# A state-space convolution beside a gated product: half of the convolution's rows sent from SBUF to SBUF in place of a round trip through DRAM

## The chip, the core and the metric

The kernel runs on one core of one Trainium2 chip. The metric is device microseconds for one execution. TensorE (PE) multiplies into PSUM, ScalarE (ACT) and VectorE (DVE) evict and combine, GpSimd (POOL) does little, SyncE (SP) issues nearly all transfers, which run on 16 DMA engines.

## What is computed

The input is one sequence of 2,048 tokens with 512 channels, in bf16. After a layernorm, two branches run on it and are added to the input:

```python
def reference(A_u, A_A_re, ..., B_w_gate, B_w_up, B_w_down):
    ...
    # _A_ref: a long convolution per channel
    P = jnp.exp(logdA[:, :, None] * l[None, None, :])
    K = jnp.einsum("dn,dnl,dn->dl", Cc, P, dB).real      # D=512, N=128, L=2048
    ...                                                  # y = causal convolution of u with K, by FFT
    y = y + u * Dskip[None, None, :]
    # _B_ref: a gated product, F = 1792
    h = _sigmoid(x @ w_gate) * (x @ w_up)
    return h @ w_down
    ...
    return x + _A_ref(xn, ...) + _B_ref(xn, ...)
```

## The kernel before

*The gated branch* is cut into four groups of 512 tokens. For each group TensorE makes 14 gate blocks (L1010) and 14 up blocks (L1034), ScalarE applies the sigmoid (L1022), VectorE multiplies (L1049), and after a group's 14 products TensorE makes four down products of 128 tokens (L1078).

*The convolution* is done in a transformed space with matmuls. Each of its two halves of the channels (p = 0 and p = 1, 256 channels each) has eight units u. Of a unit: its input rows are loaded from DRAM (z_scr), transformed (L878) and evicted; the halves of the partitions are swapped (by four 64 KB copies big<-big for p = 0, by VectorE at L891 for p = 1); the filter's spectrum is made from a loaded table E (320 KB) and the kernel's rows kT (L900) and evicted; VectorE multiplies the two (L905, L909); TensorE transforms back in part (L922, called V here); ScalarE evicts the result into one of two buffers `vs` (L926, by the helper at L286). A helper (`dma`, L420) issues every transfer.

*The closing products* (`s2_mm`, L969, matmuls at L974 and L976) contract over 128 rows: 8 units x 4 rows x 4 blocks. They need these rows on the partitions, while `vs` holds 32 time positions x 4 blocks there. The change of layout is made by a store of each unit to DRAM (v_scr) and loads into the buffer `vall`. The stores go into three tensors (VPART: the first half; six units of the second half; its last two units), and for each of four parts of time there are three loads; a closing product waits for those of its part (`vp_op`). The results are added to the gated branch's (L989 and L1098) and stored.

*Order.* The kernel is recorded as 959 steps, each with an engine, its dependences and the buffers that it takes and frees. A list written out by hand, ORDER, says in which order the steps are issued; each engine and each queue works through its own steps in this order and stops at the first that has to wait. UEV says which up blocks ScalarE evicts ahead of the product, ON_DVE which copies VectorE makes in place of ScalarE. PSUM has two buffers of two banks (`pair`) and four of one bank (`bank`).

At the end of ORDER the last two units of the second half (u = 7, then u = 6) are followed by three gate and up blocks, and then by the down products 12 to 15 with the closing products between them.

Of the kernel before, what the change touches and what calls it, by code (L numbers as in the profile page):

```python
# [10 lines left out]
BF = mybir.dt.bfloat16  # L11
F32 = mybir.dt.float32
I32 = mybir.dt.int32
ACT = mybir.ActivationFunctionType
# [63 lines left out]
def _build_S2(by):  # L78
    h = np.zeros((64, 64))
    a = np.arange(64)  # L80
    h[0, :] = 1.0 / 2048
    h[1, :] = (-1.0) ** a / 2048
    for s in range(1, 32):
        h[2 * s, :] = 2.0 / 2048 * np.cos(2 * np.pi * s * a / 64)
        h[2 * s + 1, :] = -2.0 / 2048 * np.sin(2 * np.pi * s * a / 64)
    S2 = np.zeros((128, NA))
    S2[0:64] = h
    S2[64:128, 32:64] = h[:, 0:32]
    return S2.reshape(2, NU, 4, NA).transpose(1, 0, 2, 3)[by].reshape(128, NA)
# [88 lines left out]
def _consts():  # L178
# [19 lines left out]
UEV = (0, 1, 3, 5, 6, 7, 8, 10, 12, 16, 17, 19, 21, 22, 23, 24, 26, 27, 28, 29, 30, 31, 32, 33, 34, 35, 36, 37, 38, 39, 40, 41, 42, 44, 46, 49, 52, 54,)  # L198
ON_DVE = (66, 102, 103, 119, 120, 121, 135, 136, 137, 182, 192, 193, 195, 196, 228, 364,)
ON_ACT = (2,)  # L200
ORDER = [
# [115 lines left out]
def kernel(  # L317
# [80 lines left out]
    s2 = at(OFF["tmp"], [2, 64])  # L398
    rr = at(OFF["tmp"] + KB // 2, [D])
    sr = at(OFF["tmp"] + 3 * KB // 2, [4, 64])  # L400
# [6 lines left out]
    VPART = ((0, 0, NU // 2), (1, 0, NU // 2 - 2), (1, NU // 2 - 2, NU // 2))  # L407
    k_scr = dram.tile([16, NGE, 8, 2, NKQ * 16], BF, name="k_scr")
    c_scr = dram.tile([2, 16, 2, 16], BF, name="c_scr")
    v_scr = [dram.tile([4 * (u1 - u0), 128, DW], BF, name="v_scr%d" % n) for n, (p, u0, u1) in enumerate(VPART)]  # L410
# [332 lines left out]
    for c in range(4):  # L743
# [91 lines left out]
        def f_ds(pc=pc):  # L835
# [6 lines left out]
    kgen[3][0].rel += tuple(_Slot(k, i) for k, i in (("xx", 3), ("zx", 2), ("zx", 3), ("zx", 7), ("zx", 8), ("zx", 9)))  # L842
    kgen[2][0].rel += (_Slot("zx", 5), _Slot("zx", 6))
    gcs[3].rel += (_Slot("zx", 4),)
# [9 lines left out]
                vs=[OFF["kx"] + 4 * KB, OFF["kx"] + 6 * KB], zx=[OFF["zs"], OFF["zs"] + 2 * KB] + [KB * k for k in (4, 6, 12, 18, 20, 22, 28, 30)])  # L854
# [7 lines left out]
    v_st = [[] for _ in VPART]  # L862
    for p in range(NP):
        dsl = slice(DW * p, DW * p + DW)
        for u in UNITS[p]:
# [49 lines left out]
            def fv(u=u, sv=sv, pp=pp, pq=pq):  # L915
                for n in range(4):
                    q, y = n % 2, n // 2
                    for g in range(2):
                        ch = slice(DW * g, DW * g + DW)
                        for b in (0, 64):  # L920
# [6 lines left out]
            vn = [n for n, (p_, u0, u1) in enumerate(VPART) if p_ == p and u0 <= u < u1][0]  # L927
            vo = 4 * (u - VPART[vn][1])
            v_st[vn].append(dma("SP", v_scr[vn][vo:vo + 4, :, :].rearrange("g q d -> q g d"),
                               lambda vs=vs: vs().rearrange("p g y d -> p (g y) d"), deps=[ev], prio=QP - 1, rel=[vsl],  # L930
                               pkt=512)(256 * KB))

    TAIL = dict(ot=0, xt=8 * KB, glu=OFF["G"], vall=OFF["tmp"] - 32 * KB)
    assert TAIL["glu"] + 4 * KB <= TAIL["vall"]
    k_c = [dma("SP", c_scr[:][n], k_scr[:][:, 0, 0, :, 16 * (NKT - 1 + n):16 * (NKT + n)], deps=k_st[0] + k_st[1], prio=60, pkt=32)(1 * KB)
           for n in range(2)]
# [231 lines left out]
```

## Time and profile before

| | us |
|---|---|
| median of 3 runs | 222.95 (222.6 to 225.01) |
| the profiled execution, its own time | 223.55 |
| its span in the trace | 221.6 |
| PE busy | 206.1 (93%) |
| DVE busy | 198.9 (90%) |
| ACT busy | 176.3 (80%) |

The span runs from the first to the last instruction of the trace; 1.95 us of the execution's own time lie around it. The granted clock of TensorE was 0.99 over the span. Busy shares are averages over stages with different limits, so the views by time say more: rows of 40 slices have one digit for a slice of 5.54 us, in tenths of busy time. A wait is put down to what ended it last. Matmul rows have modelled ends and overlap each other.

### The profile page before, as it was taken

The page shows a single profiled execution, that of the slowest core. Times are in us where ns is not written, and L with a number is a line of the kernel's source. Part 1 is how long each engine was busy: PE and PEld are TensorE (multiplying, and loading weights), DVE is VectorE, ACT ScalarE, POOL GpSimd, SP SyncE. Part 2 cuts the span into 40 slices and gives each one's busy share as a digit, 9 for nine tenths or more (in the row PEclk, how much of TensorE's full clock was granted, in tenths as well). Part 3 has the DMA queues.
Part 4 walks back from the last instruction along what each step waited for, and adds up shares of the span by engine and source line. Part 5 has one row for each costly group of instructions (what it writes and reads, how often), then busy time and mean ns, then how long its engine had stood idle before and what let it go on. Part 6 is the DMA issues. An engine that isn't in the chain of part 4 may idle for free. (4 is left out here: it accounts for less than half of the span.)

```text
span 221.6 us, 4849 instructions
## 1 busy us (share of the span) xinstructions
PE 206.1 (93%) x1810; PEld 102.9 (46%) x1836; DVE 198.9 (90%) x440; ACT 176.3 (80%) x282; POOL 23.7 (11%) x40
## 2 busy tenths in 40 slices
PE   7769999999999999989999999999699999999694
PEld 2344444444444454435455565463347455544243
DVE  3899998999999999999999998999988999890663
ACT  3889999999999999849999999698486898851000
POOL 2101202005800000000000000004007400000000
PEclk9979999999999999999999999999999999999999
DMA  6999824005177476546595565879786999866934
GB/s 185 340 378 376 273 95 96 0 3 189 10 227 173 135 269 157 190 115 193 126 293 147 150 172 155 239 199 276 165 230 136 296 292 245 251 189 217 261 134 151
DMA packets 51529, 42.80 MB, mean 193 GB/s; under 512 B 16433, under 2 KB 43570, under 8 KB 51506
## 3 DMA queue, kind: packets, MB, share of 16 engines
q1 hardware_dynamic: 50338, 40.60, 61.6%
q0 software_dynamic: 864, 1.57, 4.4%
q10 hardware_dynamic: 304, 0.33, 0.5%
q8 instruction: 14, 0.23, 0.5%
q14 instruction: 9, 0.07, 0.1%
HBM read 25.97 MB, written 12.85 MB: 175 GB/s over the span
## 5 line engine op out<-in xcount | busy, mean ns | idle before, releaser
L286 ACT ACTIVATE big<-pair 128x1024 bf16<-128x1024 f32 x64 | 65.2, 1043 | 9.5 <-PE pair L878 3.2
L1034 PE MATMUL bank<-xnT,wu_sb 128*128 128x512 bf16 x215 | 54.0, 379 | 0.7 <-issue 0.2
L1010 PE MATMUL bank<-xnT,wg_sb 128*128 128x512 bf16 (+1 forms) x210 | 51.3, 376 | 2.4 <-ACT xnT L568 1.7
L1078 PE MATMUL bank<-wd_sb,hT_sb 128*128 128x512 bf16 (+1 forms) x232 | 49.7, 366 | 0.6 <-issue 0.2
L1010 PEld LDWEIGHTS <-wg_sb 128*128 128x128 bf16 x236 | 22.7, 100 | 26.5 <-issue 4.8
L1078 PEld LDWEIGHTS <-hT_sb 128*128 128x128 bf16 x238 | 22.8, 98 | 25.1 <-issue 1.7
L1022 ACT ACTIVATE hT_sb<-bank 128x512 bf16<-128x512 f32 x52 | 31.0, 625 | 2.0 <-PE bank L1010 1.9
L1034 PEld LDWEIGHTS <-wu_sb 128*128 128x128 bf16 x224 | 20.9, 98 | 25.0 <-issue 2.9
L731 DVE TENSOR_TENSOR big<-big 128x1024 bf16<-128x1024 bf16 (+4 forms) x40 | 26.8, 671 | 0.2
L732 DVE TENSOR_TENSOR big<-big 128x1024 bf16<-128x1024 bf16 (+4 forms) x40 | 26.7, 667 | 0.0
L1045 ACT ACTIVATE us_sb<-bank 128x512 bf16<-128x512 f32 x38 | 23.6, 625 | 0.3 <-PE bank L1034 0.3
L905 DVE TENSOR_TENSOR big<-big 128x2048 bf16<-128x2048 bf16 x16 | 19.5, 1218 | 1.6 <-DMA big<-big 0.8
L900 PE MATMUL pair<-big 128*128 128x256 bf16 x160 | 19.8, 273 | 0.1
L900 PEld LDWEIGHTS <-big 128*128 128x128 bf16 x160 | 15.6, 98 | 4.8 <-issue 0.2
L737 DVE TENSOR_TENSOR big<-big 128x512 bf16<-128x512 bf16 (+4 forms) x40 | 16.7, 417 | 0.0
L736 DVE TENSOR_TENSOR big<-big 128x512 bf16<-128x512 bf16 (+4 forms) x40 | 16.7, 416 | 0.0
L1049 DVE TENSOR_TENSOR hT_sb<-hT_sb,us_sb 128x512 bf16<-128x512 bf16 x38 | 15.8, 419 | 0.2 <-ACT hT_sb L1022 0.2
L785 ACT ACTIVATE sq_sb<-big 128x256 bf16<-128x256 bf16 (+2 forms) x20 | 13.5, 675 | 2.4 <-DVE big L737 2.4
L891 DVE COPY big<-big 32x1024 bf16<-32x1024 bf16 x32 | 14.5, 454 | 0.5
L922 PE MATMUL pair<-big 64*64 64x512 bf16 (+1 forms) x256 | 13.0, 326 | 0.5 <-ACT big L286 0.4
L1049 DVE TENSOR_TENSOR hT_sb<-hT_sb,bank 128x512 bf16<-128x512 bf16 x18 | 12.1, 684 | 1.4 <-PE bank L1034 1.1
L658 ACT ACTIVATE big<-big 128x512 bf16<-128x512 f32 x22 | 13.2, 681 | 0.0
(99 smaller groups left out, 222.9 us busy)
## 6 DMA issues: line engine op xcount, KB each, us to landing
big<-c_E SPq DMA_DIRECT2D x16, 320.0 KB, 4.3
z_scr<-big SPq DMA_DIRECT2D x16, 256.0 KB, 2.9
big<-z_scr SPq DMA_DIRECT2D x16, 256.0 KB, 4.1
v_scr<-big SPq DMA_DIRECT2D x16, 256.0 KB, 3.7
big<-in_A_u_dram SPq DMA_DIRECT2D x4, 512.0 KB, 9.4
big<-big SPq DMA_DIRECT2D x32, 64.0 KB, 3.5
big<-v_scr SPq DMA_DIRECT2D x4, 512.0 KB, 5.5
wu_sb<-in_B_w_up_dram SPq DMA_DIRECT2D x2, 896.0 KB, 11.0
```

Source lines behind the costliest of these rows:

```text
L286: nc.scalar.activation(out=get(out), in_=get(in_), func=ACT.Identity)
L731: V.tensor_tensor(out=wide(outp), in0=wide(lo), in1=mre, op=ALU.mult)
L732: V.tensor_tensor(out=wide(tb()), in0=wide(lo), in1=mim, op=ALU.mult)
L736: V.tensor_tensor(out=outp[:, :, 0], in0=outp[:, :, 0], in1=tb()[:, :, 1], op=opr)
L900: T.matmul(two(sk)[:, o:o + DW], es()[:, g, kt, :], kTv[p][:, :, kt, :], start=kt in (0, NKT - 1), stop=kt >= NKT - 2)
L905: V.tensor_tensor(out=pp().rearrange("p q h m -> p (q h) m"), in0=xx().rearrange("p q h m -> p (q h) m"), in1=kb()[:, 0:2 * DW].unsqueeze( ...
L1010: T.matmul(bank(sl, k % 2)[:, c0:c1], w[:, kt, k * 128:(k + 1) * 128], xnT[:, grp, kt, c0:c1], start=(kt == 0), stop=(kt == KT - 1))
L1022: S.activation(out=hT_sb[:, hs.idx, k % 2, :], in_=bank(sl), func=ACT.Sigmoid)
L1034: T.matmul(bank(sl), wu_sb[:, kt, k * 128:(k + 1) * 128], xnT[:, grp, kt, :], start=(kt == 0), stop=(kt == KT - 1))
L1045: S.activation(out=us_sb[:, us.idx, :], in_=bank(sl), func=ACT.Identity)
L1049: V.tensor_tensor(out=h(), in0=h(), in1=us_sb[:, us.idx, :] if on else bank(sl), op=ALU.mult)
L1078: T.matmul(bank(po)[:, 0:c[1] - c[0]], hT_sb[:, hts[k // 2].idx, k % 2, jj * 128:(jj + 1) * 128], wd_sb[:, k, c[0]:c[1]], start=first and ...
```

## The change

The second half's results no longer go through DRAM. After the eviction into `vs`, four copies of 64 KB for each unit, one for each pair of spectrum half and block (n = 0 to 3), go from SBUF to SBUF, straight to the buffer `vall` of the closing products: from 128 partitions with 512 bytes each into four partitions (32 n + 4 u and the three after it) with 16 KB each. Of the 32 copies 28 are issued by SP, four (the odd n of the last two units) by ScalarE's queue. The buffer `vs` is free again when all four have landed. The first half keeps its store and is loaded, as before, by four transfers of 512 KB, with the rows in another order; VPART is gone. The closing matrix S2 has its rows permuted to match. `vall` lies in another place, so the small tables s2, rr and sr move to `sq_sb`, and the list of buffers for the units' input rows (`zx`) is changed, with seven late places in place of eight. UEV, ON_DVE and ORDER are written anew; there are 975 steps. In ORDER no gate or up block is left behind the last unit; the load of the input rows for the last four results (512 KB, `lx`) is issued between the copies of the last two units.

```diff
-    return S2.reshape(2, NU, 4, NA).transpose(1, 0, 2, 3)[by].reshape(128, NA)
+    return S2.reshape(2, NU, 4, NA).transpose(1, 0, 2, 3)[by].reshape(NU // 2, 4, 4, NA).transpose(1, 0, 2, 3).reshape(128, NA)
...
-UEV = (0, 1, 3, 5, 6, 7, 8, 10, 12, 16, 17, 19, 21, 22, 23, 24, 26, 27, 28, 29, 30, 31, 32, 33, 34, 35, 36, 37, 38, 39, 40, 41, 42, 44, 46, 49, 52, 54,)
-ON_DVE = (66, 102, 103, 119, 120, 121, 135, 136, 137, 182, 192, 193, 195, 196, 228, 364,)
+UEV = (0, 2, 3, 4, 5, 6, 8, 13, 17, 19, 21, 22, 23, 24, 26, 27, 28, 29, 30, 31, 32, 33, 34, 35, 36, 37, 38, 39, 40, 41, 43, 44, 45, 46, 48, 50, 51, 52, 54, 55,)
+ON_DVE = (66, 81, 101, 103, 104, 119, 120, 135, 182, 194, 195, 196,)
...
-    s2 = at(OFF["tmp"], [2, 64])
-    rr = at(OFF["tmp"] + KB // 2, [D])
-    sr = at(OFF["tmp"] + 3 * KB // 2, [4, 64])
+    s2 = sq_sb[:, 0, 0:128].rearrange("p (r n) -> p r n", r=2)
+    rr = sq_sb[:, 0, 128:128 + D]
+    sr = sq_sb[:, 1, 0:256].rearrange("p (r n) -> p r n", r=4)
...
-    VPART = ((0, 0, NU // 2), (1, 0, NU // 2 - 2), (1, NU // 2 - 2, NU // 2))
...
-    v_scr = [dram.tile([4 * (u1 - u0), 128, DW], BF, name="v_scr%d" % n) for n, (p, u0, u1) in enumerate(VPART)]
+    v_scr = dram.tile([4, NU // 2, 128, DW], BF, name="v_scr")
...
-    kgen[3][0].rel += tuple(_Slot(k, i) for k, i in (("xx", 3), ("zx", 2), ("zx", 3), ("zx", 7), ("zx", 8), ("zx", 9)))
-    kgen[2][0].rel += (_Slot("zx", 5), _Slot("zx", 6))
-    gcs[3].rel += (_Slot("zx", 4),)
+    kgen[3][0].rel += tuple(_Slot(k, i) for k, i in (("xx", 3), ("zx", 2), ("zx", 3), ("zx", 4), ("zx", 5)))
+    kgen[2][0].rel += (_Slot("zx", 7), _Slot("zx", 8))
+    gcs[3].rel += (_Slot("zx", 6),)
...
-            vn = [n for n, (p_, u0, u1) in enumerate(VPART) if p_ == p and u0 <= u < u1][0]
-            vo = 4 * (u - VPART[vn][1])
-            v_st[vn].append(dma("SP", v_scr[vn][vo:vo + 4, :, :].rearrange("g q d -> q g d"),
-                               lambda vs=vs: vs().rearrange("p g y d -> p (g y) d"), deps=[ev], prio=QP - 1, rel=[vsl],
-                               pkt=512)(256 * KB))
-
-    TAIL = dict(ot=0, xt=8 * KB, glu=OFF["G"], vall=OFF["tmp"] - 32 * KB)
+            if p == 0:
+                v_st[0].append(dma("SP", v_scr[:, u].rearrange("g q d -> q g d"),
+                                   lambda vs=vs: vs().rearrange("p g y d -> p (g y) d"), deps=[ev], prio=QP - 1, rel=[vsl],
+                                   pkt=512)(256 * KB))
+                continue
+
+            for n in range(4):
+                r0 = 32 * n + 4 * u
+                v_st[1].append(dma("ACT" if n % 2 and u in (6, 7) else "SP", vall[r0:r0 + 4, 1].rearrange("p j i d -> p (j i) d"), lambda vs=vs, n=n: vs()[:, n // 2, n % 2, :],
+                                   deps=[ev] + table_free, prio=QP - 1, rel=[vsl] if n == 3 else [], pkt=512)(64 * KB))
...
-    vall = at(TAIL["vall"], [4, NP, 2, 4, DW])
+    v_v = v_scr[:].rearrange("g u (a j i) d -> (g u a) j i d", j=2, i=NT)
     vl = []
-    for t in range(0, 8, 2):
-        lds = []
-        for n, (p, u0, u1) in enumerate(VPART):
-            v_v = v_scr[n][:].rearrange("g q d -> (g q) d").rearrange("(p j i) d -> p j i d", j=2, i=NT)
-            lds.append(dma("ACT" if n == 2 and t % 4 else "SP", vall[16 * u0:16 * u1, t // 2, p], v_v[:, :, 2 * t:2 * t + 4, :],
-                           deps=v_st[n] + table_free, prio=20 + n + 0.01 * t, pkt=2048, hv=0.9)(64 * KB * (u1 - u0)))
-        vl.append(lds)
-    vp_op = [vl[t // 2] for t in range(8)]
+    for n in range(4):
+        vl.append(dma("SP", vall[:, 0, :, 4 * n:4 * n + 4], v_v[:, :, 4 * n:4 * n + 4, :], deps=v_st[0] + table_free, prio=20 + 0.02 * n, pkt=2048,
+                      hv=0.9)(512 * KB))
+    vp_op = [[vl[t // 2]] + v_st[1] for t in range(8)]
...
-            T.matmul(o[64 * j:64 * j + 64, :], s2[:, r, :], vall[:, t // 2, ps, j, 2 * (t % 2) + r, :], start=start, tile_position=(0, 64 * j), **kw)
+            T.matmul(o[64 * j:64 * j + 64, :], s2[:, r, :], vall[:, ps, j, i, :], start=start, tile_position=(0, 64 * j), **kw)
```

More of the change, by code (lines that the diff above doesn't have):

```diff
@@ L853 @@
                 pq=[OFF["lad"] + 10 * KB, OFF["pq"]],
-                vs=[OFF["kx"] + 4 * KB, OFF["kx"] + 6 * KB], zx=[OFF["zs"], OFF["zs"] + 2 * KB] + [KB * k for k in (4, 6, 12, 18, 20, 22, 28, 30)])
+                vs=[OFF["kx"] + 4 * KB, OFF["kx"] + 6 * KB], zx=[OFF["zs"], OFF["zs"] + 2 * KB] + [KB * k for k in (0, 2, 4, 6, 12, 18, 20)])
     mab = at(OFF["lad"] + 6 * KB, [NU, 2, 64])
@@ L860, in slot @@
         return sl, lambda: at(HOME[pool][sl.idx], shape)
-    v_st = [[] for _ in VPART]
+    TAIL = dict(ot=0, xt=8 * KB, glu=OFF["G"], vall=OFF["G"] + 8 * KB)
+    assert TAIL["vall"] + 32 * KB <= OFF["W0"]
+    vall = at(TAIL["vall"], [NP, 2, NT, DW])
+    v_st = [[], []]
     for p in range(NP):
@@ L926 @@
             ev = pl.copy(nc, 0.90, lambda vs=vs: vs().rearrange("p g y d -> p (g y d)"), lambda sv=sv: two(sv), [mv_], QP, acq=[vsl], rel=[sv])
-            vn = [n for n, (p_, u0, u1) in enumerate(VPART) if p_ == p and u0 <= u < u1][0]
-            vo = 4 * (u - VPART[vn][1])
-            v_st[vn].append(dma("SP", v_scr[vn][vo:vo + 4, :, :].rearrange("g q d -> q g d"),
-                               lambda vs=vs: vs().rearrange("p g y d -> p (g y) d"), deps=[ev], prio=QP - 1, rel=[vsl],
-                               pkt=512)(256 * KB))
-    TAIL = dict(ot=0, xt=8 * KB, glu=OFF["G"], vall=OFF["tmp"] - 32 * KB)
-    assert TAIL["glu"] + 4 * KB <= TAIL["vall"]
+            if p == 0:
[7 more added lines that the diff above has]
+                                   deps=[ev] + table_free, prio=QP - 1, rel=[vsl] if n == 3 else [], pkt=512)(64 * KB))
     k_c = [dma("SP", c_scr[:][n], k_scr[:][:, 0, 0, :, 16 * (NKT - 1 + n):16 * (NKT + n)], deps=k_st[0] + k_st[1], prio=60, pkt=32)(1 * KB)
```

87 rows, old and new, of the table ORDER are left out of this document.

## The prediction

> **What bounds the kernel now.** I read the page first, then the waits of TensorE (PE), the end of the chain, TensorE's order of time at the end, and the transfers by stretches. Durations are from the one profiled execution.
>
> ```profile
> span 221.6 us, 4849 instructions
> PE 206.1 (93%) x1810; PEld 102.9 (46%) x1836; DVE 198.9 (90%) x440; ACT 176.3 (80%) x282; POOL 23.7 (11%) x40
> PE   7769999999999999989999999999699999999694
> DVE  3899998999999999999999998999988999890663
> DMA  6999824005177476546595565879786999866934
> ```
>
> TensorE and VectorE are both nearly full until about 199 us; then VectorE is mostly idle and TensorE runs the closing products. From 140 us on the transfers are full too. The waits say what TensorE's few gaps are (total, times, longest):
>
> ```profile
> PE pair L974 <- DMA big<-v_scr: 2.0, 2, 1.5
> PE pair L878 <- ACT big L286: 1.7, 1, 1.7
> PE pair L878 <- DMA big<-z_scr: 0.9, 1, 0.9
> ```
>
> The first is the round trip this change removes; the chain shows it (start, us, what):
>
> ```profile
> 196.35 1.03 ACT big L286
> ...
> 197.39 4.22 DMA v_scr<-big
> ...
> 204.22 5.42 DMA big<-v_scr
> ...
> 209.80 2.97 PE bank L1078 x13
> ...
> 218.46 0.42 DVE big L1098
> ```
>
> The last unit's rows leave ScalarE at 197.38, are in DRAM at 201.61, and the last load lands at 209.64: 12.3 us. TensorE covers nearly all of it with down products:
>
> ```profile
> 198.60 0.39 PE L951 MATMUL pair<-ident,rz 128*8 128x128 bf16 x4
> 198.92 6.22 PE L1078 MATMUL bank<-wd_sb,hT_sb 128*128 128x512 bf16 x28
> 205.57 0.62 PE L974 MATMUL pair<-big 128*64 128x512 bf16 x4 [0.43 <-DMA big<-v_scr]
> ...
> 208.59 1.05 PE L974 MATMUL pair<-big 128*64 128x512 bf16 x8 [1.53 <-DMA big<-v_scr]
> ```
>
> So of 12.3 us only 0.43 + 1.53 + 0.16 (at 209.80) = 2.12 us are idle. That is all a shorter way can give at the end. Last, the transfers (last two columns: share of the 16 DMA engines, GB/s):
>
> ```profile
> 126.00:127.00 1.00, 0.95 (x18) 0.41 (x8) 1.00 (x6) 1.00 (x3) 0.00 (x0) 1.00 1.01 290
> 180.00:185.00 5.00, 4.95 (x57) 3.10 (x56) 4.76 (x10) 4.21 (x6) 0.00 (x0) 1.00 0.96 262
> 185.00:190.00 5.00, 4.95 (x55) 2.54 (x54) 4.86 (x10) 4.67 (x6) 0.00 (x0) 1.00 0.89 223
> ```
>
> In the first stretch nearly all packets are the 512-byte ones of one v_scr store: 16 x 512 B x 1.01 / 290 GB/s = 28.5 ns a packet on its engine. The other two show that the stage where the second half's units finish has almost no transfer time to spare.
>
> **The change, part by part.** *Removed:* eight 256 KB stores and 2 MB of reloads of the second half, and the 2.12 us of waiting. Span 221.6 - 2.1 = 219.5.
>
> *Order.* TensorE's instructions are the same set. By the list ON_DVE eight small steps move from VectorE to ScalarE and four the other way, and by UEV ScalarE evicts two more up products: VectorE loses about 1.6 us net (two products at 0.42 in place of 0.68, two layernorm applications at 0.31, one key eviction at 0.87, two small copies at 0.13, less a cast of 0.67), ScalarE gains about 2.8 us, which its 20% of idle time hides. I summed the work ahead of each step on its engine in both orders: the tightest VectorE-to-TensorE step has 0.7 us more room than before. One more product stands ahead of the first unit's spectrum product, two stand behind the last key table: these can cover the gaps of 0.9 and 1.7 us. Bounds: 0 to -2.6 us; I take 0 for the sum. In exchange no product is left between the last unit's matmul and the down products (before: three, 2.6 us).
>
> *Added:* each of eight units sends four copies of 64 KB, SBUF to SBUF, from 128 partitions x 512 B into **four** partitions x 16 KB. Issue: 28 on SP at 0.58 us (the row of the 32 copies big<-big) against 8 stores at 0.38 and six loads at 0.63 less; four on ScalarE's queue in place of two (0.66 to 0.99 us each there); two of these stand ahead of the last eviction, whose matmul comes 2.6 us later, so they are hidden. New waits: an eviction now waits for the four copies of the unit two before it (two vs buffers), with sigmoids and the other evictions queued behind it on ScalarE, and TensorE behind those for a PSUM pair. On SP the filter loads of the last two units (E, 320 KB) stand behind copies.
>
> No row shows a transfer into four partitions. Low end: 128 packets over 16 engines, 8 x 28.5 ns = 0.23 us a copy, landing about 2 us after issue as the copies into 32 partitions do in light traffic (105.97 to 108.05). High end: these copies into 32 partitions already pay: their 2 KB packets take a median of 147 ns (106.0 to 108.7 us, packet records), packets of that size into 128 partitions 84. By the same rate for each destination partition (64 KB in two rounds of 147 ns, 7 GB/s a partition) four partitions take 28 GB/s: 2.35 us a copy. I take one DMA engine for each destination partition, which lies between: 32 packets x 28.5 ns = 0.91 us a copy, **3.65 us a unit** on the same four engines, 29.2 us for eight, where the stores cost each engine 0.91 us a unit. The one-partition load in the trace (dskr, 1 KB) went as a single packet, so a transfer needn't use all engines.
>
> [...]
>
> **The sum.** The first copies are issued at about 175.6 (before: the first such store, 175.58). Ahead of the last copies the four engines must also do: what is queued already, about 3 us (transfers issued at 169 to 172 landed 7 to 8 us later); two E loads (8 packets of 102 ns each, 0.8 us each); two reloads of the first half (16 x 84 ns, 1.35 us each); the x load moved here (8 x 160 ns, 1.3 us); the SR load, 0.3. That is 8.9 us, and 29.2 for the copies: 213.7, landed 1.5 us later, 215.2. TensorE then has what it had from 205.57 on without its waits: 218.44 - 205.57 - 1.53 - 0.16 = 11.2 us, to 226.4; from there 3.1 us to the end (218.46 to 221.6): span 229.5, **7.9 us more**. The execution's own time was 223.55 for 221.6 of span, 231.5 for this one; the runs' median, 222.95, lies 0.6 lower, so 231. Own range: 226.5 (nothing queued, 27 ns packets) to 236 (5 us queued, queue at times empty).
>
> **Rivals.**
> - *Faster: the copies land like others.* Their price is the low end; TensorE's next step needs them at 198.6 + 0.39 + 6.22 = 205.2, they are there at about 203 (eviction to 199.7, two issues of 0.58, 2.0 to land). Span 219.5, 220.8 as a run; with the gaps of 0.9 and 1.7 closed 218.2. I take 220. It decides up to about 0.4 us a copy. For it: 512-byte packets take 27 to 28 ns whether loaded or stored, and there are 2 MB less to move. Against it: the 147 ns packets into 32 partitions.
> - *The partitions limit, not the engines.* The high end: 2.35 us a copy, 9.4 a unit, 75 for eight: 46 us more than above, 277; if two pairs of copies, into different quarters of the partitions, run side by side, half of 75: 8 us more, 239. For it: the same 147 ns. Against it: those copies also read only 32 partitions.
> - *The wait takes the removed one's place.* Price as for stores: landing 4.2 us after issue, behind the x load (1.3): 206.4 against 205.2 needed, so 1.2 us of the 2.1 come back: 222.
>
> [...]
>
> **How the numbers follow.** Forecast 0.36; copies harmless 0.25; partitions limit 0.32 (half of it side by side); replaced wait 0.07. A measurement of this kernel can tell about 1% from no change: below 220.7 is faster, above 225.2 slower. Faster: most of the harmless case, 0.21. Same: its rest, 0.04, and the replaced wait, 0.06: 0.10. Slower: 0.69. The range reaches from the harmless case with one gap closed, 218.5, to 262; beyond lies the serial half of the partitions' case.
>
> **What would show it.** Right: four-partition copies that land 5 us or more after issue, DMA share well under 0.9 while SP and ScalarE wait for them, L286 waiting for big<-big, TensorE idle before the last V products (L922's line) and before S2 (L974's), no wait longer than before ahead of 170 us. Wrong: copies landing in 2 to 3 us with TensorE unbroken from 199 us on; or new gaps before 170 us, which would make it the order.

## The result and the profile after

The changed kernel takes 260.7 us in the median (258.6 to 263.9) against 223.9 for the kernel before on the same chip: 1.161 times, interval 1.149 to 1.174. The forecast was 231: the direction holds, the loss is between four and five times as large (36.8 us in place of 8). Runs of one kernel differ by one or two per cent, the longer ones mostly at a lower granted clock, so the ratios leave the disturbed runs out, and the medians given beside them can lie a microsecond or two off.

The page of the profiled execution, to be read against the same rows of before (span 221.6, PE 206.1):

```profile
span 258.1 us, 4904 instructions
PE 217.3 (84%) x1836; PEld 106.6 (41%) x1836; DVE 197.4 (76%) x437; ACT 180.1 (70%) x287; POOL 21.5 (8%) x40
PE   7589999998999998999999998999909567830595
PEclk9869999999999999999999999999986955995589
DMA  6999340148713587877876877667464352446234
```

Up to about the 29th slice (187 us) TensorE is nearly as full as before. After it TensorE has holes, its granted clock drops (0.66 from 190 to 200), and the transfers take up half of the 16 engines' time (0.48 to 0.50 from 180 to 210). Before, the same stage looked like this (busy us of PE, PEld, DVE, ACT and POOL; last three columns: granted clock, share of the 16 DMA engines, GB/s):

```profile
180.00:190.00 10.00, 9.90 (x110) 5.64 (x110) 9.62 (x19) 8.88 (x12) 0.00 (x0) 1.00 0.93 243
190.00:200.00 10.00, 9.90 (x77) 4.98 (x78) 8.47 (x18) 6.21 (x9) 0.00 (x0) 1.00 0.75 231
200.00:210.00 10.00, 7.88 (x43) 3.48 (x43) 3.11 (x4) 0.59 (x1) 0.00 (x0) 1.00 0.79 235
```

A half-empty transfer row beside engines that wait for transfers needs a closer look. By the packet records, the 512-byte packets, nearly all of them the copies', fill 0.20 to 0.29 of the 16 engines in the 10 us stretches from 180 to 240, about four engines' worth (0.25). The waits in the changed kernel (total, times, longest; lines that do not bear on the copies left out):

```profile
...
ACT big L287 <- DMA big<-big: 22.3, 4, 8.1
...
DVE big L908 <- ACT big L287: 18.9, 4, 10.1
...
PE pair L976 <- DMA big<-big: 13.6, 1, 13.6
PE pair L925 <- ACT big L287: 10.0, 2, 6.7
...
PE pair L903 <- DMA big<-c_E: 4.2, 2, 3.7
```

big<-big is the copies. They hold TensorE at the closing products (L976), ScalarE at the evictions (L287: two row buffers, so an eviction waits for the copies of the unit two before), and through ScalarE TensorE again (L925) and VectorE (L908). The filter loads (c_E) are late behind them. The three TensorE waits are 27.8 us, of which before had 2.4; TensorE's busy time is 11.2 longer for the same products (217.3 against 206.1; 1,836 weight loads in both, though the trace of before lacks 26 of the matmul records). 27.8 - 2.4 + 11.2 = 36.6, nearly the 36.5 us between the two spans; the other waits come out about even. The chain that ended last shows the same: of the 59.3 us from 181.7 to 241.0, 40.7 are copies:

```profile
181.70 10.58 DMA big<-big
192.52 1.03 ACT big L287
...
200.61 12.52 DMA big<-big
213.27 1.03 ACT big L287
...
222.73 10.00 DMA big<-big
233.41 7.61 DMA big<-big
241.47 1.06 PE pair L976 x4
```

The stretches (last three columns: granted clock, share of the 16 DMA engines, GB/s) say where the extra busy time is:

```profile
190.00:200.00 10.00, 6.40 (x38) 3.17 (x37) 4.10 (x7) 6.02 (x8) 0.00 (x0) 0.66 0.49 99
200.00:210.00 10.00, 6.33 (x54) 3.33 (x54) 3.83 (x10) 2.35 (x4) 0.00 (x0) 0.78 0.48 77
210.00:220.00 10.00, 6.71 (x43) 2.34 (x41) 2.50 (x4) 2.92 (x4) 0.00 (x0) 0.54 0.30 58
220.00:230.00 10.00, 6.67 (x40) 2.94 (x32) 0.69 (x1) 3.12 (x4) 0.00 (x0) 1.00 0.50 83
230.00:240.00 10.00, 0.00 (x0) 0.00 (x0) 0.00 (x0) 0.00 (x0) 0.00 (x0) 0.64 0.58 78
240.00:250.00 10.00, 8.53 (x41) 4.23 (x43) 4.78 (x5) 0.00 (x0) 0.00 (x0) 0.67 0.32 116
```

Once TensorE begins to wait, the granted clock is 0.54 to 0.78 in four of the five stretches up to 240 and 0.67 in the next; before it was 1.00 from 180 to 210. Busy time times the clock that was not granted, summed over the stretches from 190 to 250, gives an estimate of 9.5 us, most of the 11.2. So the loss shows twice here: as idle time, and in slower products around it. Whether the waiting itself lowers the clock was not tested.

How many engines a copy uses can be estimated from the packets of four bytes that the traces hold. In the kernel with nothing but copies (below), four of them follow a copy into four partitions, and the 400 packets under 512 B on its page are what four for each such copy, eight for a copy into eight partitions and 16 for every other transfer add up to. That one such packet stands for one engine is the author's reading. The times of a copy into partitions four apart agree with it: its 128 packets of 28 ns are 3.6 us and were over in 0.9, four at a time. Before, after, and the later kernel with copies into eight partitions (one line of each page):

```profile
DMA packets 51529, 42.80 MB, mean 193 GB/s; under 512 B 16433, under 2 KB 43570, under 8 KB 51506
```
```profile
DMA packets 50377, 40.70 MB, mean 158 GB/s; under 512 B 16305, under 2 KB 43442, under 8 KB 50354
```
```profile
DMA packets 50505, 40.71 MB, mean 168 GB/s; under 512 B 16433, under 2 KB 43570, under 8 KB 50482
```

The change makes 16 more transfers. At 16 such packets each, as other transfers leave, the count under 512 B should rise by 256; it falls by 128, so the 32 copies leave 384 too few, 12 each: four engines a copy. Into eight partitions the count doesn't change (16433), so it is 8 too few for each copy: eight engines. Into 16 and into 32 partitions it rises by exactly 256 (16689): 16 engines.

### The profile page after: what moved, and what is told of

Read it like the earlier page. It is cut to its first block, busy times and chain, and to the rows that moved or that the text cites. A ratio compares the mean times of both kernels' runs of the same rounds, so it can differ in the third digit from the quotient of the medians.

```text
span 258.1 us, 4904 instructions
## 1 busy us (share of the span) xinstructions
PE 217.3 (84%) x1836; PEld 106.6 (41%) x1836; DVE 197.4 (76%) x437; ACT 180.1 (70%) x287; POOL 21.5 (8%) x40
## 2 busy tenths in 40 slices
DMA packets 50377, 40.70 MB, mean 158 GB/s; under 512 B 16305, under 2 KB 43442, under 8 KB 50354
## 4 chain that ended last, share of the span: by engine, by line
PE 39%; DVE 28%; DMA 19%; ACT 5%; POOL 2%; SPq 2%; issue 2%; ACTq 1%; DVEq 0%
DMA big<-big 16%; PE bank L1036 9%; PE bank L1012 8%; PE bank L1080 7%; DVE big L732 6%; DVE big L731 6%; PE pair L903 5%; PE pair L925 4%; DVE hT_sb L1051 4%; DVE big L737 3%; DVE big L736 3%; ACT big L287 2%; SPq L420 2%; PE pair L976 2%; POOL ln_ve_b L476 2%
## 5 line engine op out<-in xcount | busy, mean ns | idle before, releaser
L287 ACT ACTIVATE big<-pair 128x1024 bf16<-128x1024 f32 x64 | 65.0, 1033 | 32.0 <-DMA big<-big 22.3
L1036 PE MATMUL bank<-xnT,wu_sb 128*128 128x512 bf16 x224 | 56.1, 388 | 1.3 <-ACT big L287 1.3
L1012 PE MATMUL bank<-xnT,wg_sb 128*128 128x512 bf16 (+1 forms) x220 | 54.3, 389 | 1.1 <-ACT xnT L568 1.1
L1080 PE MATMUL bank<-wd_sb,hT_sb 128*128 128x512 bf16 (+1 forms) x238 | 50.5, 367 | 0.1
L908 DVE TENSOR_TENSOR big<-big 128x2048 bf16<-128x2048 bf16 x16 | 19.5, 1221 | 20.4 <-ACT big L287 18.9
L903 PE MATMUL pair<-big 128*128 128x256 bf16 x160 | 21.4, 288 | 4.3 <-DMA big<-c_E 4.2
L925 PE MATMUL pair<-big 64*64 64x512 bf16 (+1 forms) x256 | 14.4, 351 | 10.0 <-ACT big L287 10.0
L903 PEld LDWEIGHTS <-big 128*128 128x128 bf16 x160 | 16.4, 103 | 10.5 <-DMA big<-c_E 5.5
L976 PE MATMUL pair<-big,sq_sb 128*64 128x512 bf16 x24 | 6.6, 509 | 13.6 <-DMA big<-big 13.6
L991 DVE TENSOR_TENSOR big<-pair,big 128x1024 bf16<-128x1024 f32 x2 | 2.4, 1224 | 20.3 <-PE pair L976 20.1
L1051 DVE TENSOR_TENSOR hT_sb<-hT_sb,us_sb 128x512 bf16<-128x512 bf16 x40 | 16.7, 421 | 1.0 <-ACT us_sb L1047 0.9
L736 DVE TENSOR_TENSOR big<-big 128x512 bf16<-128x512 bf16 (+4 forms) x40 | 16.6, 416 | 0.1
L737 DVE TENSOR_TENSOR big<-big 128x512 bf16<-128x512 bf16 (+4 forms) x40 | 16.6, 415 | 0.0
L925 PEld LDWEIGHTS <-big 64*64 64x64 bf16 x256 | 7.3, 112 | 19.7 <-issue 16.7
```

Source lines behind the costliest of these rows:

```text
L287: nc.scalar.activation(out=get(out), in_=get(in_), func=ACT.Identity)
L736: V.tensor_tensor(out=outp[:, :, 0], in0=outp[:, :, 0], in1=tb()[:, :, 1], op=opr)
L737: V.tensor_tensor(out=outp[:, :, 1], in0=outp[:, :, 1], in1=tb()[:, :, 0], op=opi)
L903: T.matmul(two(sk)[:, o:o + DW], es()[:, g, kt, :], kTv[p][:, :, kt, :], start=kt in (0, NKT - 1), stop=kt >= NKT - 2)
L925: T.matmul(two(sv)[o:o + 64, DW * (2 * g + y):2 * DW * (g + 1)], mab[b:b + 64, 2 * u + g, q, :], pq()[b:b + 64, q, ch] if y else pp()[b:b ...
L1012: T.matmul(bank(sl, k % 2)[:, c0:c1], w[:, kt, k * 128:(k + 1) * 128], xnT[:, grp, kt, c0:c1], start=(kt == 0), stop=(kt == KT - 1))
```

## The experiments

**Order or copies?** Two halves of the change, each alone. First the new order, engine lists and buffers with the way through DRAM kept:

```diff
-  n in range(4): dma(vall[r0:r0 + 4, 1] <- vs[:, n])
+  dma(v_scr <- vs); later dma(vall <- v_scr)      # order, UEV, ON_DVE of the changed kernel
```

> The new order of work, the new lists of which engine evicts what and the new buffers, but the second half's rows go through DRAM as before the change: what the order costs by itself. Order theory (the copies are cheap, the new order is what costs): 250 us or more. Copies theory (any form of it): the changed kernel was only 2.6 us behind at its last key table, 158 us into the span, so 222 to 227 us, 0 to +1.5% against before. Middle: 225.

232.6 us, 1.043 (1.035 to 1.051): between what the two theories said, and what neither foresaw. The longest of TensorE's waits tells part of why:

```profile
PE pair L932 <- DMA big<-v_scr: 5.7, 2, 4.3
```

The new order has no product left between the last unit and the down products, so the DRAM trip that it does not expect to make stands open for 5.7 us in place of 2.0. That is 3.7 of the 8.8 us between the two spans; the rest is not explained here. This run prices the order with a transfer that it was not made for, not the order itself. The other half, the copies with the order and lists of before:

```diff
-UEV, ON_DVE, ORDER of the changed kernel
+UEV, ON_DVE, ORDER of the kernel before (copies put where the stores were)
```

> The opposite half: the copies of the changed kernel with the order and the engine lists of before. Copies theory: nearly the whole loss, 250 to 262 us. Order theory: 219 to 226 us. If the two only harm together: well under 250 here and under 227 in the run with the order alone.

261.7 us, 1.163 (1.145 to 1.181): the whole loss, with the order of before. The copies are the cause.

**Four partitions, or the copies as such?** The same number of copies, bytes and waits, spread wider:

```diff
-vall[r0:r0 + 4, 1]                          # r0 = 32 n + 4 u, 4 partitions x 16 KB
+vall[32 * n:32 * n + 32, 1][4 u: 4 u + 4]   # 32 partitions x 2 KB
```

> The changed kernel with each 64 KB copy going into 32 partitions x 2 KB in place of four x 16 KB: the same number of copies, bytes, waits and issues. The rows then land in another place of the buffer, so the closing products read other rows of the second half (same shapes, same instructions). Four-partition theories (either the four engines or the way into four neighbour partitions is the limit): the loss goes nearly all away, 221 to 230 us. Count-and-waits theory (32 more copies with their latency, two row buffers and an issue queue that waits in order): unchanged, 252 to 262 us. My forecast's price (0.91 us a copy on four engines becomes 0.23 on 16) would give about 222 to 226.

228.0 us, 1.014 (1.006 to 1.022). Count, issue and waits of 32 copies cost about 3 us; that each goes into only four partitions costs the other 33.

**Engines or partitions?** Four engines a copy either way, but partitions four apart:

```diff
-r0 = 32 * n + 4 * u;  vall[r0:r0 + 4, 1]
+vall[16 * u + n:16 * u + 16:4, 1]           # and rows of the first half and of the final sum to match
```

> The changed kernel with the rows numbered so that each copy still goes into four partitions, but into partitions four apart (r, r+4, r+8, r+12) in place of four neighbours; the first half's reloads go to every fourth partition, 512 KB each, the final sum reads its axes in the matching order. Engine theory (four engines carry each copy, whatever the partitions): unchanged within 2%, 255 to 263 us. Theory of a shared way into neighbour partitions: a copy is up to four times as fast, 222 to 235 us. Theory of a limit of each single partition: unchanged.

249.6 us, 1.119 (1.111 to 1.127), in the gap between the stated outcomes. The copies' 512-byte packets took 29 ns in the mean against 54 in the changed kernel, so neighbours do matter; but the reloads of the first half had become 16 KB packets (784 ns in the median), and TensorE's longest waits are put down to them (11.1 us at the filters' products). Repeated without that side effect:

```diff
-vall[r0:r0 + 4, 1]
+vall[16 * u + n:16 * u + 16:4, 1]           # nothing else
```

> The changed kernel with one edit: each copy goes into four partitions four apart (16u+n, +4, +8, +12) instead of four neighbours; the first half's loads stay as they are (in the run with partitions apart above they had become 16 KB packets of 0.6 to 1.7 us, which held the copies up). The closing products then read the second half's rows in another order; shapes and instructions are the same. In the changed kernel the copies' 512-byte packets take 54 ns in the mean, in the earlier run with partitions apart 29 ns. If the packets are 29 ns again and the four engines are the only limit, they need 29.7 us in place of some 55 for the copies: 25 us less, 232 to 238 us. If waits between the units set the pace: 245 to 252, as before. If partitions four apart gain only through the changed loads: 258 to 262.

234.6 us, 1.040 (1.031 to 1.048): some 26 of the 37 us are gone with the number of engines unchanged (16305 packets under 512 B, as in the changed kernel). Stretches and TensorE's waits of this kernel:

```profile
180.00:190.00 10.00, 8.76 (x81) 5.13 (x82) 8.58 (x15) 8.16 (x11) 0.00 (x0) 1.00 0.51 148
190.00:200.00 10.00, 7.33 (x77) 3.96 (x77) 5.81 (x15) 5.60 (x8) 0.00 (x0) 1.00 0.50 140
```
```profile
PE pair L976 <- issue: 4.2, 1, 4.2
PE pair L925 <- ACT big L287: 3.0, 2, 2.5
```

The transfer share is the same half as in the changed kernel, at about one and a half times the GB/s (148 and 140 in place of 93 and 99): as many engines, but each packet short (30 ns in the mean against 54). The wait at L976, from 210.3 to 214.5, is listed as "issue", but it is still the one for the copies: the semaphore that TensorE waits for gets its last four landings, those of the last copy, from 213.9 to 214.2. Then 16 and eight neighbours:

```diff
-vall[r0:r0 + 4, 1]
+vall[32 n + 16 (u % 2): + 16, 1][8 (u // 2): + 8]     # 16 partitions x 4 KB
+vall[32 n + 8 (u % 4): + 8, 1][16 (u // 4): + 16]     # other run: 8 partitions x 8 KB
```

> The changed kernel with each copy going into 16 neighbouring partitions x 4 KB (the closing products read the second half's rows in another order). Engine count as the limit: 16 engines as with 32 partitions, packets of 27 to 31 ns, 225 to 230 us. [...]

> The same with eight neighbouring partitions x 8 KB. Engine count alone (eight engines, 29 ns packets): 0.46 us a copy, 14.9 us for all 32, which the work between units hides: 226 to 231 us. Partitions alone (eight neighbours at twice the rate of four): half of the changed kernel's loss against the copies into 32 partitions, 240 to 246 us. [...]

228.9 us, 1.016 (1.009 to 1.023), and 241.2 us, 1.070 (1.061 to 1.079). Side by side:

| a copy goes into | engines | groups of four neighbours | ratio to before |
|---|---|---|---|
| 4 neighbours (the change) | 4 | 1 | 1.161 |
| 8 neighbours | 8 | 2 | 1.070 |
| 4, four apart | 4 | 4 | 1.040 |
| 16 neighbours | 16 | 4 | 1.016 |
| 32 neighbours | 16 | 8 | 1.014 |

Eight engines on two groups of neighbours do worse than four engines on four (1.070 against 1.040): how the partitions lie is the first limit. Counting in groups of four is the author's choice; no run tried two or three neighbours, and none shows what neighbours share. With four groups each, 16 engines gain 5.7 us over four (234.6 - 228.9): the engines are the second. (The four copies of a unit share one block of 16 partitions in the run four apart, and have a block each in the run with 16 neighbours, so this pair alone does not prove it; the run with nothing but copies bears it out.) The expectation for copy8p by engines alone (226 to 231) is refuted.

**The disputed cost by itself.** A kernel with nothing but copies, each waited for by a small VectorE step:

> No part of the computation but the copies: 64 KB from 128 partitions (512 bytes each), one at a time, three times over into four neighbouring partitions, four partitions four apart, 8, 16 and 32 neighbours, each waited for before the next is issued; then groups of four copies (a unit's) into four groups of neighbours in different quarters, into four partitions four apart within one block of 16, all four into the same four neighbours, and into 32 partitions each. From the changed kernel's packet records (97 to 121 ns a packet and 22 to 30 GB/s where one copy ran alone, 27 to 29 ns with partitions apart): four neighbours 2.2 to 3.0 us of packets (64 KB at 22 to 30 GB/s), four apart 0.9 us, 8 neighbours 1.1 to 1.5, 16 and 32 neighbours 0.25 to 0.7; four copies into the same four neighbours 9 to 12 us, into different quarters 3 to 9, four apart 3.7. If the neighbours are no limit by themselves and the long packets come from other traffic: 0.9 us for four neighbours too.

The steps of one round, in the order four neighbours, four apart, 8, 16 and 32 neighbours (in brackets, from the step before until the copy has landed):

```profile
39.94 0.30 DVE L340 COPY src<-dst 128x128 bf16<-128x128 bf16 x1 [4.46 <-DMA dst<-src]
42.79 0.30 DVE L340 COPY src<-dst 128x128 bf16<-128x128 bf16 x1 [2.54 <-DMA dst<-src]
46.31 0.30 DVE L340 COPY src<-dst 128x128 bf16<-128x128 bf16 x1 [3.22 <-DMA dst<-src]
49.09 0.30 DVE L340 COPY src<-dst 128x128 bf16<-128x128 bf16 x1 [2.48 <-DMA dst<-src]
51.66 0.30 DVE L340 COPY src<-dst 128x128 bf16<-128x128 bf16 x1 [2.27 <-DMA dst<-src]
...
80.57 0.30 DVE L340 COPY src<-dst 128x128 bf16<-128x128 bf16 x1 [12.08 <-DMA dst<-src]
86.00 0.30 DVE L340 COPY src<-dst 128x128 bf16<-128x128 bf16 x1 [5.13 <-DMA dst<-src]
99.18 0.30 DVE L340 COPY src<-dst 128x128 bf16<-128x128 bf16 x1 [12.88 <-DMA dst<-src]
103.72 0.30 DVE L340 COPY src<-dst 128x128 bf16<-128x128 bf16 x1 [4.24 <-DMA dst<-src]
```

The last four are groups of four copies: neighbours in four quarters, four apart, all into the same neighbours, 32 partitions. One copy more into neighbours costs (12.08 - 4.46) / 3 = 2.5 us, one more into partitions four apart (5.13 - 2.54) / 3 = 0.86. Nothing else ran, so other traffic is not the reason. The packet records of the groups: 87 to 101 ns a packet and 25.6 to 28.1 GB/s for neighbours, 28 ns and 76 to 78 GB/s four apart. 28 ns is what 512-byte packets take elsewhere in these kernels (27 to 28), so four apart the four engines work without a gap and are the limit.

**A dose.** Half the copies:

```diff
-for n in range(4):
+for n in (0, 2):
```

> The changed kernel without the copies n = 1 and 3 of each unit: 16 copies in place of 32 (half of the second half's rows are not moved, all waits on the others stay). If the four engines are a queue that always has work, what the copies cost is their engine time: half of 55 us, 27.5, about what 32 copies into partitions four apart took (29.7 us, 234.6): 231 to 237 us. If the waits from unit to unit set the pace (an eviction waits for the copies of the unit two before it): 245 to 256, since each unit still waits for two slow copies. If only the other traffic slows them: 245 to 255 too.

238.5 us in the median of four runs (232.9 to 239.9), too few to give an interval. That is well below what waits from unit to unit were expected to give (245 to 256); the shortest run lies within what a queue that always has work gives (231 to 237), the others 1 to 3 us above. The cost goes mostly with the number of copies. But each unit also waits for two copies in place of four here, so the two theories are not fully told apart.

**What a harmless copy is worth.** Copies into 32 partitions with the order of before:

```diff
 ORDER, UEV, ON_DVE of the kernel before
+vall[32 * n:32 * n + 32, 1][4 u: 4 u + 4]
```

> The copies into 32 partitions x 2 KB with the order and engine lists of before (closing products read the second half's rows in another order): what a harmless copy would be worth. My forecast's first rival: the 2.1 us of waiting at the end go, 0.985 to 0.995 of before. If the new order costs nothing and the three microseconds seen with it come from the copies: 1.01 to 1.02, as with the new order. If the copies still collide with the loads: 1.00 to 1.03.

227.0 us, 1.015 (1.010 to 1.020), the same as with the new order (1.014), so between the two orders no difference can be seen once the transfer fits them. But the copies are not harmless even here. TensorE's waits, then its closing part and the copies on SP's queue:

```profile
PE pair L860 <- DMA big<-c_E: 3.1, 2, 1.9
...
PE pair L882 <- ACT big L244: 1.5, 2, 0.8
```
```profile
203.74 6.22 PE L1037 MATMUL bank<-wd_sb,hT_sb 128*128 128x512 bf16 x28
209.89 0.62 PE L933 MATMUL pair<-big,sq_sb 128*64 128x512 bf16 x4
```
```profile
176.05 6.18 SPq L377 DMA_DIRECT2D big<-big  x8
182.33 0.53 SPq L377 DMA_DIRECT2D big<-c_E  x1
...
185.61 7.11 SPq L377 DMA_DIRECT2D big<-big  x8
```

The waits of the closing products are gone, as forecast: they follow the down products at once. But the down products start at 203.74 where they started at 198.92: 4.8 us later, 3.1 of them in waits for filters (c_E) and 1.5 for evictions. Eight copies hold SP for 6 to 7 us, and the filter loads stand behind them. The span is 224.4, 2.8 over before: 4.8 lost, 2.0 regained. Moving two filter loads ahead of the copies:

```diff
-u4.copies, u1.copies, ... u5.E, reload 2, u6.E, u7.E
+u5.E, u6.E, u4.copies, u1.copies, ... u7.E, reload 2
```

> The copies into 32 partitions with the order of before, and on SP's queue the filter loads of the two last-but-one units moved ahead of the first eight copies and one 512 KB reload of the first half moved behind the last filter load. In the run without this TensorE waits 1.2 and 1.9 us for these filters, which were issued up to 7 us later behind the copies. If that is where the remaining 3 us (1.015) went: 0.995 to 1.005 of before. If the transfers as a whole are the limit (the wait only moves): 1.01 to 1.02.

227.7 us, 1.010 (1.006 to 1.014), at the lower end of the second stated outcome (1.01 to 1.02). The waits for filters are no longer among TensorE's longest, and the one for evictions (L882) has grown from 1.5 to 3.3:

```profile
PE pair L882 <- ACT big L244: 3.3, 3, 2.4
```

The wait mostly moves. Whether half a per cent was won can't be said, since the intervals overlap.

**A version that beats both?** Only the last units by copies, everything else as before:

```diff
+if u in (6, 7): n in range(4): dma(vall[16 u + 4 n: + 4, 1] <- vs[:, n])    # neighbours
```

> The kernel before, with its order, where only the last two units of the second half go by four copies each into four neighbouring partitions and the other six keep the way through DRAM; result complete. By my forecast's price (0.91 us a copy) the last copy lands about 203, before TensorE needs it at 205.2, and the 2.1 us of waiting go: 0.99 of before. At the price seen in the changed kernel (54 ns a packet, 1.7 us a copy, 6.9 us for the last unit's four from 198 on, landing at 206 to 207): 0.99 to 1.00. With the unit before it still in the queue: 1.01 to 1.03.

232.4 us, 1.033 (1.026 to 1.039), just above the worst of the three outcomes. Eight copies hold SP from 199.1 to 206.7, the last reloads stand behind them, and those end last:

```profile
PE pair L938 <- DMA big<-v_scr: 6.6, 1, 6.6
```

Then only the very last unit, into partitions four apart:

```diff
+if last unit: n in range(4): dma(vall[96 + n:112:4, 1] <- vs[:, n])
```

> The kernel before, with its order, where the very last unit of the second half alone goes by four copies, into four partitions four apart; all others keep the way through DRAM (the first half's store of the unit with that number is cut into four of 64 KB). Result complete. Copied alone, such a group of four took 5.1 us from issue to landing in the run with nothing but copies, so from 197.4 to about 202.5, before TensorE needs it at 205.2: the 2.1 us of waiting go, 0.985 to 0.995 of before. If the copies queue behind the loads still open on their four engines (some 1.4 MB, 4 us): 206 to 207, 0.995 to 1.005. If the other loads now end last because they are issued 2.3 us later: 1.00 to 1.01.

227.8 us, 1.016 (1.009 to 1.022): no gain, and above all three stated outcomes. The copies themselves are in time (their last packets end at 202.3); the reloads of the other units, issued from 199.92 on in place of 197.80, are now what TensorE waits for:

```profile
197.40 2.48 SPq L380 DMA_DIRECT2D big<-big  x4
199.92 7.10 SPq L380 DMA_DIRECT2D big<-v_scr  x5
```
```profile
PE pair L946 <- DMA big<-v_scr: 1.8, 1, 1.8
```

The profile is of the shortest of its six runs (224.2 us), whose span of 222.3 is only 0.7 over before; the median says 3 us, and where the others lose the rest was not found. No version tried beats the kernel before.

## Why the prediction was wrong in size

- *The term that failed: 0.91 us a copy, "one DMA engine for each destination partition, 32 packets x 28.5 ns".* No row of before shows one engine for each partition, always the same four, nor the 1.5 us to landing. The engines came out right: by the four-byte packets four a copy, and four copies four apart together still moved about four packets at a time (512 of 28 ns in the 3.4 us that 256 KB take at 76 to 78 GB/s). From the last copy's last packet to its landings it took 0.2 to 0.5 us four apart, 2.2 to 2.5 with neighbours. The 28.5 ns were wrong: they came from a store to DRAM, and with four neighbours as destination the packets took 54 ns in the mean in the kernel, 87 to 101 in the kernel with copies alone. Copies ran from about 180 to 240 us, 60 us for 32 or 1.9 each, where the sum had 29.2 us. TensorE could go on at 241.5 in place of the sum's 215.2, and from there to the end took 16.6 us in place of 14.3, at a granted clock of 0.67 at first: 26.3 + 2.3 is the whole difference between the span of 258.1 and the sum's 229.5.
- *The rest of the sum came out, in part by luck.* With partitions four apart, where 30 ns a packet were measured, the sum's last copy "landed 215.2" and its span of 229.5 met 214.5 (when TensorE goes on) and 230.1. So the working fits another layout: a limit of the destination was left to the second rival. But the sum put the whole loss into one wait ahead of the closing products, from 205.2 to 215.2; in that run TensorE waited only 4.2 us at this place and had lost the rest earlier: its down products began at 204.3 in place of 198.9. The queue of the copies set the end either way.
- *The second rival had the price, but not the unit.* Its 2.35 us a copy, from the 147 ns packets into 32 partitions, is nearly the 2.5 us measured alone. It spoke of a rate for each destination partition (7 GB/s); four partitions four apart took 76 to 78 GB/s together, four neighbours 25.6 to 28.1, so what limits is that they are neighbours. The time came between its two ends (239 and 277): in the changed kernel a copy cost 1.9 us, less than alone. That copies into different quarters of the partitions overlapped in part would fit, but in the kernel with copies alone they did not (12.1 us for four), so the reason stays open. The measured 260.7 lies inside the forecast's wide range (to 262) only because this rival was in it. I had taken the value between the two ends on a count of engines that no row showed; the nearest row in kind, the only copies from SBUF to SBUF in the trace, pointed to the high end.
- *Order at nothing:* right as far as the runs can tell; the ratios are equal with both orders, 1.161 and 1.163 with the change's copies, 1.014 and 1.015 with wide ones.
- *Two queues named and costed at nothing.* That evictions wait for the copies of the unit two before, and that filter loads stand behind copies on SP, was in the working without a price. In the changed kernel they are the 10.0 and 4.2 us at L925 and L903; with wide copies still 1.5 and 3.1. So the first rival, harmless copies at 220, fails too: cheap copies came to 227.
- *The 2.12 us of waiting* can be had, and were, with wide copies; they don't pay for what the copies delay before.
- *Not foreseen:* the granted clock, 0.92 over the span in place of 0.99. In the changed kernel TensorE was busy 11.2 us longer with its own products.
- *A reading too strong:* "from 140 us on the transfers are full too". In stretches of 10 us from 140 to 200 their share was 0.72 to 1.01 before.
- The signs named beforehand came: DMA share well under 0.9 while ScalarE waits for big<-big, TensorE idle ahead of the last V products and of the closing products, no wait of TensorE ahead of 170 us longer than before (1.7 us at most in both), copies that land 5 us or more after issue (7.6 to 12.5 us in the chain).

## What to carry to other kernels

Before a transfer replaces a trip through DRAM, look at how many partitions its destination has and how they lie: copies into four neighbours cost more here than the trip (260.7 us against 223.9), copies of the same bytes into 32 partitions hardly more (228.0). Price it from the nearest transfer of the same kind in the trace, or measure it alone, before building a sum on a packet time taken elsewhere. And price every transfer that stands behind the new ones on an in-order queue: 32 small copies in place of eight stores and eight of the reloads cost about 3 us here even when each was cheap.

## What was not expected of the hardware

- In the kernel with copies alone, four engines (by the four-byte packets) writing into four neighbouring partitions reach 25.6 to 28.1 GB/s together; into four partitions four apart 76 to 78. Putting the four copies of a unit into different quarters of the partitions hardly helped (12.1 us against 12.9 for all into the same four): by their four-byte packets they ended one after the other, 2.6 to 2.9 us apart.
- The packet records understate such a copy: one alone into neighbours had its packets over in 1.25 us (40 ns in the mean), but was seen as landed 2.0 us after one into partitions four apart, whose packets took 0.9 us. In the changed kernel the last copy's packets end at 238.5 and its four landings come from 240.7 to 241.0; with partitions four apart it is 213.7, and 213.9 to 214.2. What happens between the last packet and the landing no run here shows.
- In the kernels with many copies on four or eight engines, the pages list no time to landing for any transfer issued by SP, and a wait can be listed as "issue" (the 4.2 us at L976); with copies on 16 engines they list it.
- The granted clock fell to 0.54 to 0.78 in four of the five 10 us stretches from 190 us on, in which TensorE stood idle a third of the time or more; in the fifth, idle just as long, it was 1.00. With copies into partitions four apart, where TensorE was 73 to 88% busy from 180 to 200, it stayed at 1.00 there and was 0.83 from 200 to 210, where TensorE was 98% busy. So the clock does not simply follow the idle time of the same 10 us, and that the waiting is the cause was not tested by itself.
